# Order of ScalarE's Mish and of VectorE's sums in a fused linear attention and Mish MLP kernel

## The chip, the cores and the metric

The kernel runs on one NeuronCore of a Trainium2 chip. The metric is the time of one execution on the device, in microseconds. Engines are called as in the profile: PE is TensorE (PEld its weight loads), ACT is ScalarE, DVE is VectorE, POOL is GpSimd, and SP issues DMAs.

## What is computed

Decayed linear attention in blocks, with a state per batch and head, and then a two-layer MLP with Mish between the layers:

```python
B, H, S, D = 4, 8, 768, 64          # 3072 tokens, d_model 512, d_ff 2048
for b in range(S // 64):
    intra = einsum('bhij,bhjd->bhid', einsum('bhic,bhjc->bhij', qb, kb) * Dmask, vb)
    inter = einsum('bhid,bhde->bhie', qb * lam_pow, kv_state)
    out[:, :, block] = intra + inter
    kv_state = lam_block * kv_state + einsum('bhsd,bhse->bhde', kb * rev_pow, vb)
x = out.transpose(0, 2, 1, 3).reshape(B * S, H * D)
h = x @ w_in
g = h * tanh(log1p(exp(h)))         # Mish
return g @ w_out
```

Inputs and output are float32; the kernel works in float16 with float32 accumulation.

## The kernel before

**Periods.** The sequence is cut in six groups of 128 positions. A period n (0 to 5) takes one group of all four batches, 512 tokens, through the MLP, and works on the attention of the next group in between. Every engine's order is written out by hand: lists of `units`, and tables that say behind which unit u a token sum (`sums`), a transposition of q and k by DMA (`turns`), a load, or a part of the attention (`visit`) stands.

**First layer.** The hidden values are kept in hsg, 16 row blocks of 128 by 512 tokens. *Lower* tokens are the columns 0 to 255 (batches 0 and 1), *upper* ones 256 to 511. In period 0 (`mm1_unit`, L423) and period 1 all 16 row blocks are plain products. From period 2 on, row blocks 0 to 7 are plain: `mm1_duo(n, g, lo, hi)` (L444) makes two row blocks for one half of the tokens in one of the two PSUM banks of tag ph, and ACT applies Mish (L460). Row blocks 8 to 15 come from `set_unit` (L520), two sets g = 0, 1 of a scheme with seven block products instead of eight, P1 to P7. It needs sums of quarters of w_in (`in_sum`, made once in period 0) and of x (`x_sum`, L502: four DVE sums a period; P5 reads sum 0, P6 sum 1, P7 sum 2, P3 sum 3). Its steps, with the tiles that the profile names:

- P1 makes sx; ACT copies it to u (L576). P2 adds to sx; its Mish gives lower tokens, first columns.
- "open": ACT copies u into the bank of sz (L554), so that P6 adds to it.
- P5 makes sw; ACT copies it to p (L580).
- "mid": DVE adds sz and p into the bank of sy (L539).
- P7 adds to sz; DVE adds p into hs (L539); the Mish of hs (L535) gives upper tokens, second columns.
- P3 adds to sy; its Mish gives **lower** tokens, second columns.
- P4 adds to sz; its Mish gives **upper** tokens, first columns.

**Second layer.** `fast_unit` (L681) is the same scheme over hsg and w_out: tiles x, w, z, y, all made at L621. It needs sums of w_out (`weight_sum`, L471, tile tsum, made once in period 0) and of hsg (`token_sum`, L592, tile gsum, each in two parts, every period). Token sum 0 adds upper tokens of both halves of the row blocks; sum 1 takes from it lower tokens of row blocks 0 to 7; sum 2 uses row blocks 0 to 7 alone; sum 3 takes sum 1 from lower tokens of row blocks 8 to 15. The order in a period is P1 (x), P5 (w, reads sum 0), P6 (z, sum 1), P2 (x), P7 (z, sum 2), P3 (y, sum 3), P4 (z).

**Attention.** In `pair_s` (L338) PE makes the scores of two batches in four banks (tile pS, L349), and DVE masks them (tile sb, L365). `pair_o` (L368) multiplies by v; the result, xtok, is transposed by two DMAs from SP into xt (L392), which is what the next period's x sums and first layer read. In periods 2 to 4, the `pair_s` behind unit 3 stands just before the four x sums, which are behind unit 4. Up to the start of period 1 the scores are made batch by batch (`look_t`, `look_s`, L204 to L240) with transposes on PE (tiles pk, pq) and masks at L239.

**Pacing.** GpSimd delays loads of later groups: `pace` (L408) reads one element of the Mish output named last in `mark`.

Of the kernel before, what the change touches and what calls it, by code (L numbers as in the profile page):

```python
# [9 lines left out]
AF = mybir.ActivationFunctionType  # L10
# [10 lines left out]
def kernel(  # L21
# [10 lines left out]
    nc = tc.nc  # L32
# [408 lines left out]
        if hsg[n] is None:  # L441
            hsg[n] = work.tile([128, NKI, GT], F16, name="hsg", tag="hsg", bufs=2)

    def mm1_duo(n, g, lo, hi):  # L444

        new_hidden(n)
        h = GT // 2
        half = lo // h
        t = duo_bank(n, g, half)
        for m in range(2):  # L450
            ni = 2 * g + m
            for kc in range(NKC):
                nc.tensor.matmul(  # L453
                    t[:, m, lo - half * h : hi - half * h],
                    w_in(ni, kc),
                    xt[n][:, kc, lo:hi], start=(m == 0 and kc == 0), stop=(kc == NKC - 1),
                    skip_group_check=True,
                )
        if hi == half * h + h:
            nc.scalar.activation(hsg[n][:, 2 * g : 2 * g + 2, half * h : half * h + h], t, AF.Mish)  # L460
            mark.append(hsg[n][0:1, 2 * g, half * h : half * h + 1])

    HK = NKI // 2
    HN = DMO // 2
# [55 lines left out]
    def set_unit(n, g, step):  # L520

        def place(key):
            if (n, g, key) not in first:
                tag, bufs = homes[g][key]
                first[n, g, key] = ps.tile([128, 2, 2 * C], F32, name=f"s{key}{g}", tag=tag, bufs=bufs)
            return first[n, g, key]

        def kept(key):
            first[n, g, key] = work.tile([128, 2, 2 * C], F32, name=key, tag=key, bufs=2)
            return first[n, g, key]  # L530

        def mish(r, c, src):
            ni = NKI // 2 + 4 * g + 2 * c
            dst = hsg[n][:, ni : ni + 2, r * 2 * C : (r + 1) * 2 * C]
            nc.scalar.activation(dst, src, AF.Mish)  # L535
            mark.append(dst[0:1, 0, 0:1])

        def plus_p5(key, out):
            nc.vector.tensor_tensor(out=out, in0=first[n, g, key], in1=first[n, g, "p5"], op=ALU.add)  # L539

        def x_quarter(r, c):
            return lambda kk: xt[n][:, c * KH + kk, r * 2 * C : (r + 1) * 2 * C]

        def x_part(i):
            return lambda kk: xsum[n, i][:, kk, :]

        def w_quarter_(r, c):
            return lambda kk, m: i_quarter(g, r, c)[:, kk, m * 128 : (m + 1) * 128]

        def w_part_(i):  # L550
            return lambda kk, m: isum[g][i][:, kk, m * 128 : (m + 1) * 128]

        if step == "open":
            nc.scalar.activation(place("z"), first[n, g, "u1"], AF.Copy)  # L554
            return
        if step == "mid":
            plus_p5("z", place("y"))
            return
        key, lhs, rhs = {
            "P1": lambda: ("x", w_quarter_(0, 0), x_quarter(0, 0)),  # L560
            "P2": lambda: ("x", w_quarter_(1, 0), x_quarter(0, 1)),
            "P6": lambda: ("z", w_part_(1), x_part(1)),
            "P5": lambda: ("w", w_part_(0), x_part(0)),
            "P7": lambda: ("z", w_part_(2), x_part(2)),
            "P3": lambda: ("y", w_quarter_(1, 1), x_part(3)),
            "P4": lambda: ("z", w_part_(3), x_quarter(1, 1)),
        }[step]()
        t = place(key)
        for m in range(2):
            for kk in range(KH):  # L570
                nc.tensor.matmul(  # L571
                    t[:, m, :], lhs(kk, m), rhs(kk),
                    start=(step in ("P1", "P5") and m == 0 and kk == 0), stop=(kk == KH - 1),
                    skip_group_check=True)
        if step == "P1":
            nc.scalar.activation(kept("u1"), t, AF.Copy)  # L576
        elif step == "P2":
            mish(0, 0, t)
        elif step == "P5":
            nc.scalar.activation(kept("p5"), t, AF.Copy)  # L580
        elif step == "P7":
            o = work.tile([128, 2, 2 * C], F32, name="hs", tag="hs", bufs=2)
            plus_p5("z", o)
            mish(1, 1, o)
        elif step == "P3":
            mish(0, 1, t)
        elif step == "P4":
            mish(1, 0, t)

# [165 lines left out]
    units += [(fast_unit, (0, step, blk)) for step in ("P1", "P5") for blk in range(2)]  # L755
    units += [(fast_unit, (0, step, None, part)) for part in range(2) for step in ("P6", "P2")]
    units += [(fast_unit, (0, step, blk)) for step in ("P7", "P3", "P4") for blk in range(2)]
    sums = {3: ((2, 0),), 7: ((2, 1),), 11: ((0, 0), (1, 0), (3, 0)), 15: ((0, 1), (1, 1)), 16: ((3, 1),)}
    for u, (fn, args) in enumerate(units):
        put_off = []  # L760
        fn(*args, **({"then": put_off} if u in (23, 25) else {}))
        if u < B - 1:
            look_kv(u + 1, "pq" if u == 0 else "po")()
        if 8 <= u < 8 + NVB - B:
            nc.vector.memset(vz[u - 8 + B][:, :, D : 2 * D], 0.0)
        elif u == 13:
            nc.vector.tensor_scalar(out=maskT, in0=rel, scalar1=0.0, scalar2=None, op0=ALU.is_ge)
        for i, s in {14: ((0, 0),), 15: ((0, 1),), 18: ((1, 0), (2, 0)),
                     20: ((1, 1), (2, 1))}.get(u, ()):
            weight_sum(i, s)  # L770
        for i, part in sums.get(u, ()):
            token_sum(0, i, part)
        if u in (5, 8):
            for i in range(4):
                in_sum((u - 5) // 3, i)
        if u == 22:
            scale_k(4)
            weight_sum(3, 0)
        then = [f(i, "po" if i == 5 else "ph") if f is look_kv else f(i) for f, i in visit.get(u, ())]
        if u == 23:  # L780
            scale_k(5)
            scale_k(6)
            weight_sum(3, 1)
        for f in put_off + then:
            if f:
                f()
        if u in (25, 26, 27):
            for _ in range(2):
                ahead.pop(0)()
        if u == 26:  # L790
            scale_k(7)
    next_state(1, 0)

    for n in range(1, NG):
        r, s, t = Pair(), Pair(), Pair()
        r.n, r.bs, s.n, s.bs, t.n, t.bs = n, (2, 3), n + 1, (0, 1), n + 1, (2, 3)
        def duo(g, half):
            return mm1_duo, (n, g, half * (GT // 2), (half + 1) * (GT // 2))

        def part(g, *steps):  # L800
            return [(set_unit, (n, g, step)) for step in steps]
# [6 lines left out]
        if n == 1:  # L808
            units = [[duo(g, half)] for half in range(2) for g in range(NKI // 2)]
            visit = {11: (pair_s, s), 16: (pair_o, s), 21: (pair_a, s), 26: (pair_s, t), 29: (pair_o, t)}  # L810
            turns = {1: 9, 4: 10, 7: 11, 23: 12, 25: 13}
            slots = range(8, 16)
            sums = {9: ((2, 0),), 11: ((2, 1),), 13: ((0, 0), (1, 0)), 15: ((0, 1), (1, 1)), 20: ((3, 0),), 21: ((3, 1),)}
        else:
            units = [part(0, "P1") + part(1, "P1") + [duo(0, 0)], part(0, "P2") + part(1, "P2") + [duo(1, 0)],
                     [duo(2, 0)], [duo(3, 0)],
                     [duo(0, 1)], part(0, "open") + [duo(1, 1)], part(1, "open") + [duo(2, 1)],
                     part(0, "P5") + part(1, "P5"), part(0, "P6", "mid") + part(1, "P6"), [duo(3, 1)] + part(1, "mid"),
                     part(0, "P7") + part(1, "P7"), part(0, "P3") + part(1, "P3"),
                     part(0, "P4") + part(1, "P4")]  # L820
            if n == NG - 1:
                units[0] += units[1].pop(),
            visit = {}
            if n < NG - 1:
                visit = {0: (pair_a, r), 3: (pair_s, s), 13: (pair_o, s), 22: (pair_s, t), 25: (pair_o, t)}
            if n < NG - 2:
                visit[17] = pair_a, s
            turns = {1: (n + 1) * B + 2, 2: (n + 1) * B + 3, 20: (n + 2) * B, 23: (n + 2) * B + 1}
            slots = range(4, 16)
            sums = {9: ((2, 0),), 12: ((0, 0), (0, 1), (1, 0), (1, 1)), 14: ((2, 1),), 18: ((3, 0),), 19: ((3, 1),)}  # L830
# [3 lines left out]
        for u, calls in enumerate(units):  # L834
# [17 lines left out]
                token_sum(n, i, part)  # L852
            if turns.get(u, NG * B) < NG * B:
                turn(turns[u])
            if u in visit:
                f, s_ = visit[u]
                s_.spare = ("po", "po") if u < 13 else ("pS", "pk") if f is pair_a else ("ph", "po")
                if f is pair_o and s_ is s and n > 1:
                    f(s_, scales)
                else:  # L860
                    f(s_)
            if n > 1 and scales and u in (15, 16, 17, 19):
                scales.pop(0)()
            if n > 1 and u == 4:
                for i in range(4):
                    x_sum(n, i)


# [28 lines left out]
```

## Time and profile before

| | |
|---|---|
| median of 3 runs | 201.27 us (200.77 to 201.43) |
| the profiled execution's own time | 200.91 us |
| its span, first to last instruction | 199.1 us |
| granted TensorE clock | 1.0 of full speed |
| DMA moved | 26.82 MB |

The profile is of one execution; its span is 1.8 us shorter than that execution's time. In the timelines below a line gives the start, the length, the engine, the line of the kernel, the operation, output and inputs, shapes and a count; in brackets stands how long the engine was idle before it, and what ended that. Matmuls are pipelined: a row of eight lasts longer than the distance to the next group's start, so the text compares starts.

### The profile page before, as it was taken

The page shows a single profiled execution, that of the slowest core. Times are in us where ns is not written, and L with a number is a line of the kernel's source. Part 1 is how long each engine was busy: PE and PEld are TensorE (multiplying, and loading weights), DVE is VectorE, ACT ScalarE, POOL GpSimd, SP SyncE. Part 2 cuts the span into 40 slices and gives each one's busy share as a digit, 9 for nine tenths or more (in the row PEclk, how much of TensorE's full clock was granted, in tenths as well). Part 3 has the DMA queues.
Part 4 walks back from the last instruction along what each step waited for, and adds up shares of the span by engine and source line. Part 5 has one row for each costly group of instructions (what it writes and reads, how often), then busy time and mean ns, then how long its engine had stood idle before and what let it go on. Part 6 is the DMA issues. An engine that isn't in the chain of part 4 may idle for free.

```text
span 199.1 us, 5098 instructions
## 1 busy us (share of the span) xinstructions
PE 191.6 (96%) x2049; PEld 157.5 (79%) x2049; DVE 144.8 (73%) x279; ACT 110.8 (56%) x230; POOL 80.8 (41%) x129
## 2 busy tenths in 40 slices
PE   7978999999999999999999999999999999999993
PEld 3555447878888998988798988798988788888782
DVE  7689679799953978888589788589788538225813
ACT  5685665332665521567881557980657880787330
POOL 7996333679397810008980008970009000000000
PEclk9999999999999999999999999999999999999999
DMA  9999999999999996759999959999969714600014
GB/s 132 145 149 192 206 206 200 157 169 181 200 137 178 164 123 173 180 88 94 129 111 196 201 121 107 126 114 190 179 140 113 50 26 135 158 3 2 0 56 158
DMA packets 112458, 26.82 MB, mean 135 GB/s; under 512 B 101554, under 2 KB 112434, under 8 KB 112434
## 3 DMA queue, kind: packets, MB, share of 16 engines
q0 software_dynamic: 77552, 13.37, 91.7%
q1 hardware_dynamic: 30848, 9.97, 27.1%
q10 hardware_dynamic: 4034, 3.15, 5.6%
q8 instruction: 16, 0.26, 0.6%
q14 instruction: 8, 0.07, 0.1%
HBM read 27.26 MB, written 6.29 MB: 169 GB/s over the span
## 4 chain that ended last, share of the span: by engine, by line
PE 88%; ACT 5%; DVE 4%; issue 1%; ACTq 0%
PE ph L453 20%; PE z L621 14%; PE x L621 10%; PE ph L418 7%; PE w L621 6%; PE y L621 6%; PE sz L571 4%; PE sx L571 4%; PE pS L349 2%; PE pO L376 2%; PE pO L255 2%; PE sw L571 1%; ACT hsg L535 1%; PE pv L328 1%; PE sy L571 1%; PE busy L157 1%
## 5 line engine op out<-in xcount | busy, mean ns | idle before, releaser
L453 PE MATMUL ph<-xt,win 128*128 128x256 f16 x384 | 45.1, 273 | 0.0
L621 PEld LDWEIGHTS <-gsum 128*128 128x128 f16 x384 | 36.2, 98 | 7.3 <-DVE gsum L607 2.7
L453 PEld LDWEIGHTS <-win 128*128 128x128 f16 x384 | 37.1, 98 | 4.5
L460 ACT ACTIVATE hsg<-ph 128x512 f16<-128x512 f32 x48 | 28.6, 595 | 14.8 <-PE ph L453 14.6
L409 POOL COPY paced<-hsg 1x1 f16<-1x1 f16 x42 | 11.9, 284 | 54.8 <-ACT hsg L460 54.5
L621 PEld LDWEIGHTS <-hsg 128*128 128x128 f16 x272 | 26.0, 98 | 3.2
L607 DVE TENSOR_TENSOR gsum<-hsg 128x1024 f16<-128x1024 f16 x24 | 16.2, 688 | 14.2 <-ACT hsg L535 8.6
L621 PE MATMUL x<-wout,hsg 128*128 128x256 f16 x192 | 23.7, 273 | 0.0
L621 PE MATMUL z<-tsum,gsum 128*128 128x256 f16 x192 | 23.6, 273 | 0.0
L67 POOL DMA_DIRECT2D kn<-in_k_dram x23 | 20.5, 892 | 6.1 <-DMA win<-in_moe_w_in_dram 2.2
L78 POOL DMA_DIRECT2D vz<-in_v_dram x24 | 21.1, 884 | 4.3 <-DMA wout<-in_moe_w_out_dram 1.7
L75 POOL DMA_DIRECT2D qn<-in_q_dram x23 | 20.4, 886 | 6.0 <-DMA wout<-in_moe_w_out_dram 3.6
L365 DVE TENSOR_TENSOR sb<-pS,maskT 128x512 f16<-128x512 f32 x32 | 19.8, 683 | 1.9 <-PE pS L349 1.8
L678 ACT ACTIVATE osum<-z 128x512 f32<-128x512 f32 x5 | 3.0, 597 | 25.1 <-PE z L621 25.1
L265 DVE TENSOR_TENSOR ktil<-kn,lk 128x512 f16<-128x512 f16 (+1 forms) x22 | 14.6, 685 | 1.7 <-DMA kn<-in_k_dram 1.7
L288 DVE TENSOR_TENSOR raw<-pv,state 64x256 f32<-64x256 f32 x24 | 10.1, 422 | 6.5 <-PE pv L328 6.1
L418 PE MATMUL ph<-xt,win 128*128 128x512 f16 x64 | 14.5, 379 | 0.3 <-ACT xt L257 0.3
L571 PEld LDWEIGHTS <-isum 128*128 128x128 f16 x128 | 12.5, 97 | 2.1
L430 ACT ACTIVATE hsg<-ph 128x512 f16<-128x512 f32 x16 | 9.6, 597 | 5.8 <-PE ph L418 5.8
L621 PE MATMUL w<-tsum,gsum 128*128 128x256 f16 x96 | 12.2, 273 | 0.6 <-DVE gsum L607 0.4
L418 PEld LDWEIGHTS <-win 128*128 128x128 f16 x64 | 6.1, 98 | 7.3 <-issue 0.4
L621 PE MATMUL y<-wout,gsum 128*128 128x256 f16 x96 | 11.8, 273 | 0.0
(113 smaller groups left out, 307.9 us busy)
## 6 DMA issues: line engine op xcount, KB each, us to landing
vz<-in_v_dram POOLq DMA_DIRECT2D x24, 128.0 KB, 4.4
out_dram<-osum SPq DMA_DIRECT2D x12, 256.0 KB, 2.9
kn<-in_k_dram POOLq DMA_DIRECT2D x23, 128.0 KB, 5.0
qn<-in_q_dram POOLq DMA_DIRECT2D x23, 128.0 KB, 5.7
out_dram<-osum ACTq DMA_DIRECT2D x11, 256.0 KB, 3.1
wout<-in_moe_w_out_dram POOLq DMA_DIRECT2D x4, 512.0 KB, 16.1
win<-in_moe_w_in_dram POOLq DMA_DIRECT2D x3, 512.0 KB, 10.7
win<-in_moe_w_in_dram POOLq DMA_DIRECT2D x2, 256.0 KB, 6.8
```

What stands on the lines that cost most here:

```text
L67: nc.gpsimd.dma_start(out=kn[i], in_=chunk_rows(k, i))
L75: nc.gpsimd.dma_start(out=qn[i], in_=chunk_rows(q, i))
L78: nc.gpsimd.dma_start(out=vz[i % NVB][:, :, 0:D], in_=chunk_rows(v, i))
L265: (nc.gpsimd if B + 1 < i < 2 * B else nc.vector).tensor_tensor(out=t, in0=kn[i], in1=bc(lk, 2, D), op=ALU.mult)
L365: nc.vector.tensor_tensor(out=s.sb[m][t], in0=sc[m][t], in1=bc(maskT, 1, JP), op=ALU.mult)
L409: nc.gpsimd.tensor_copy(paced, mark[-1])
L418: nc.tensor.matmul(ph_t[ni][:, lo:hi], w_in(ni, kc), xt[n][:, kc, lo:hi], start=(kc == 0), stop=(kc == NKC - 1),)
L453: nc.tensor.matmul(t[:, m, lo - half * h : hi - half * h], w_in(ni, kc), xt[n][:, kc, lo:hi], start=(m == 0 and kc == 0), stop=(kc == NKC ...
L460: nc.scalar.activation(hsg[n][:, 2 * g : 2 * g + 2, half * h : half * h + h], t, AF.Mish)
L571: nc.tensor.matmul(t[:, m, :], lhs(kk, m), rhs(kk), start=(step in ("P1", "P5") and m == 0 and kk == 0), stop=(kk == KH - 1), skip_group_c ...
L607: nc.vector.tensor_tensor(out=gsum[n, i][:, ks, :], in0=a, in1=b, op=op)
L621: nc.tensor.matmul(places(n, key)[:, blk, lo:hi], lhs(kk, blk), rhs(kk, lo, hi), start=(fresh and kk == 0 and blk == 0), stop=(kk == HK - ...
```

## The change

Five edits; no operation is added or removed, only the place of some on ACT and DVE changes (and line numbers by up to 8). PE, POOL and SP issue the same instructions in the same order.

1. Periods 2 to 5: the Mish behind P3 (lower tokens, both sets) goes behind the Mish behind P4 (upper tokens, both sets).
2. Periods 2 to 5: the Mish of `mm1_duo` for row blocks 4 and 5, upper tokens, goes behind ACT's copy p of set 0.
3. Periods 2 to 4, where `pair_s` stands behind unit 3: x sum 0 is made before the masks of `pair_s`; sums 1 to 3 stay behind unit 4. In period 5 there are no masks, and the order of the sums stays.
4. Period 0: token sum 3, second part, goes from behind unit 16 to behind unit 21, on DVE behind four sums of w_out.
5. Period 0: `weight_sum(3, 1)` goes from behind the first `look_t` of unit 23 to unit 22.

```diff
-    def mm1_duo(n, g, lo, hi):
+    def mm1_duo(n, g, lo, hi, put_off=False):
...
-        if hi == half * h + h:
-            nc.scalar.activation(hsg[n][:, 2 * g : 2 * g + 2, half * h : half * h + h], t, AF.Mish)
-            mark.append(hsg[n][0:1, 2 * g, half * h : half * h + 1])
+        if hi == half * h + h and not put_off:
+            duo_mish(n, g, half)
+
+    def duo_mish(n, g, half):
+        h = GT // 2
+        dst = hsg[n][:, 2 * g : 2 * g + 2, half * h : half * h + h]
+        nc.scalar.activation(dst, duo_t[n, g, half], AF.Mish)
+        mark.append(dst[0:1, 0, 0:1])
...
+        if step == "late":
+            mish(0, 1, first[n, g, "y"])
+            return
...
-        elif step == "P3":
-            mish(0, 1, t)
...
-    sums = {3: ((2, 0),), 7: ((2, 1),), 11: ((0, 0), (1, 0), (3, 0)), 15: ((0, 1), (1, 1)), 16: ((3, 1),)}
+    sums = {3: ((2, 0),), 7: ((2, 1),), 11: ((0, 0), (1, 0), (3, 0)), 15: ((0, 1), (1, 1)), 21: ((3, 1),)}
...
         if u == 22:
             scale_k(4)
             weight_sum(3, 0)
+            weight_sum(3, 1)
...
             scale_k(6)
-            weight_sum(3, 1)
...
-                     [duo(0, 1)], part(0, "open") + [duo(1, 1)], part(1, "open") + [duo(2, 1)],
-                     part(0, "P5") + part(1, "P5"), part(0, "P6", "mid") + part(1, "P6"), [duo(3, 1)] + part(1, "mid"),
+                     [duo(0, 1)], part(0, "open") + [duo(1, 1)], part(1, "open") + [(mm1_duo, (n, 2, GT // 2, GT, True))],
+                     part(0, "P5") + [(duo_mish, (n, 2, 1))] + part(1, "P5"), part(0, "P6", "mid") + part(1, "P6"), [duo(3, 1)] + part(1, "mid"),
                      part(0, "P7") + part(1, "P7"), part(0, "P3") + part(1, "P3"),
-                     part(0, "P4") + part(1, "P4")]
+                     part(0, "P4") + part(1, "P4") + part(0, "late") + part(1, "late")]
...
+            if n > 1 and u == 3:
+                x_sum(n, 0)
             if u in visit:
...
             if n > 1 and u == 4:
-                for i in range(4):
+                for i in range(1, 4):
                     x_sum(n, i)
```

## Prediction

> **What bounds the kernel now.** I read the page first, then the waits of the weight loads, then the timelines of the engines around each place where TensorE stood still.
>
> ```profile
> span 199.1 us, 5098 instructions
> ...
> PE 191.6 (96%) x2049; PEld 157.5 (79%) x2049; DVE 144.8 (73%) x279; ACT 110.8 (56%) x230; POOL 80.8 (41%) x129
> ```
>
> ```profile
> PEld L621 <- DVE gsum L607: 2.7, 8, 0.7
> ```
>
> TensorE is busy for 96% of the span. No matmul is removed, so only its gaps can be won. The second answer, from the waits, names the largest repeated one: weight loads of the second product waited eight times for a sum of hidden tiles. For the rest I compare starts. Eight matmuls of 128x256 that wait for nothing take 0.87 us from start to start (91.63 to 92.51 below), 0.109 us each; what goes beyond is a gap.
>
> Period 5 shows the wait for the sum best: ScalarE, VectorE, TensorE.
>
> ```profile
> 181.52 1.23 ACT L535 ACTIVATE hsg<-hs 128x512 f16<-128x512 f32 x2 [0.69 <-DVE hs L539]
> 182.66 1.06 ACT L535 ACTIVATE hsg<-sy 128x512 f16<-128x512 f32 x2
> 183.61 1.09 ACT L535 ACTIVATE hsg<-sz 128x512 f16<-128x512 f32 x2
> ...
> 184.24 1.29 DVE L607 TENSOR_TENSOR gsum<-hsg 128x1024 f16<-128x1024 f16 x2 [2.16 <-ACT hsg L535]
> ...
> 182.66 1.91 PE L621 MATMUL x<-wout,hsg 128*128 128x256 f16 x16
> 184.99 2.09 PE L621 MATMUL w<-tsum,gsum 128*128 128x256 f16 x16 [0.42 <-DVE gsum L607]
> ```
>
> The sum reads the upper tokens' Mish, hs and sz; sy, the lower tokens', stands between them. The x matmuls would end at 182.66 + 16 x 0.109 = 184.41; w begins at 184.99, 0.58 late, and is 2.09 long against x's 1.91: another 0.18 for the sum's second half. Together 0.76 us.
>
> Period 2 is the pattern of periods 2 to 4: TensorE, VectorE, ScalarE.
>
> ```profile
> 88.03 2.79 PE L453 MATMUL ph<-xt,win 128*128 128x256 f16 x24
> 90.76 1.03 PE L571 MATMUL sw<-xsum,isum 128*128 128x256 f16 x8
> 91.63 1.04 PE L571 MATMUL sz<-xsum,isum 128*128 128x256 f16 x8
> 92.51 1.04 PE L453 MATMUL ph<-xt,win 128*128 128x256 f16 x8
> ...
> 95.17 1.08 PE L571 MATMUL sz<-xt,isum 128*128 128x256 f16 x8
> ...
> 97.43 1.04 PE L621 MATMUL x<-wout,hsg 128*128 128x256 f16 x8
> 98.51 1.76 PE L621 MATMUL w<-tsum,gsum 128*128 128x256 f16 x13
> ...
> 87.89 2.49 DVE L365 TENSOR_TENSOR sb<-pS,maskT 128x512 f16<-128x512 f32 x4 [0.59 <-PE pS L349]
> 90.30 0.42 DVE L514 TENSOR_TENSOR xsum<-xt 128x512 f16<-128x512 f16 x1
> ...
> 97.76 1.29 DVE L607 TENSOR_TENSOR gsum<-hsg 128x1024 f16<-128x1024 f16 x2 [2.16 <-ACT hsg L535]
> ...
> 89.88 0.60 ACT L554 ACTIVATE sz<-u 128x512 f32<-128x512 f32 x1 [0.17 <-DVE sb L365]
> ...
> 90.89 0.59 ACT L554 ACTIVATE sz<-u 128x512 f32<-128x512 f32 x1
> 91.41 0.58 ACT L460 ACTIVATE hsg<-ph 128x512 f16<-128x512 f32 x1
> 91.89 1.08 ACT L580 ACTIVATE p<-sw 128x512 f32<-128x512 f32 x2
> ```
>
> x would end at 97.43 + 0.87 = 98.30; w begins 0.21 later and, with the same two halves of a sum as in period 5, loses the same 0.18 inside: 0.39. The ph group would end at 88.03 + 24 x 0.109 = 90.65; sw, which reads the first x sum (begun at 90.30, behind the masks), begins 0.11 later. The row at 95.17 is 1.08 where its like has 1.04: 0.05 of waiting for VectorE; the sz group before it I take as the same.
>
> Third, the boundary of periods 0 and 1: VectorE, TensorE.
>
> ```profile
> 34.82 0.68 DVE L480 TENSOR_TENSOR tsum<-wout,tsum 128x1024 f16<-128x1024 f16 x1
> ...
> 37.92 0.69 DVE L480 TENSOR_TENSOR tsum<-wout,tsum 128x1024 f16<-128x1024 f16 x1
> 39.71 0.69 DVE L219 TENSOR_TENSOR pqT<-pq,lq 128x512 f16<-128x512 f16 x1 [1.11 <-PE pq L211]
> ...
> 40.92 0.69 DVE L480 TENSOR_TENSOR tsum<-wout,tsum 128x1024 f16<-128x1024 f16 x1
> 41.52 1.28 DVE L239 TENSOR_TENSOR sb<-pS,maskT 128x512 f16<-128x512 f32 x2
> ...
> 33.67 1.91 PE L621 MATMUL w<-tsum,gsum 128*128 128x256 f16 x16
> 35.56 1.05 PE L621 MATMUL z<-tsum,gsum 128*128 128x256 f16 x8
> ...
> 40.81 1.05 PE L621 MATMUL z<-tsum,gsum 128*128 128x256 f16 x8
> 42.26 0.38 PE L211 MATMUL pk<-ident,ktil 128*128 128x128 f16 x4 [0.40 <-DVE sb L239]
> ```
>
> w would end at 35.42; z begins 0.14 later, after the sum of w_out of 34.82. The z of 40.81 would end at 41.68; pk begins 0.58 later, when the first mask (41.52) has read that bank. Ahead of the masks stands the sum of w_out of 40.92.
>
> **The change part by part.**
>
> *Sums of period 0.* weight_sum(3, 1), 0.69 us, goes from 40.92 to behind 37.92, into the 1.11 us for which VectorE waits at 39.71: hidden. The hidden sum that stands just ahead of 34.82 goes behind the four sums of w_out after it; its reader y comes after 42.26: hidden. One such sum holds VectorE for 0.60 us (40.92 to 41.52), so that of 34.82 begins 0.6 earlier and the 0.14 goes. The masks begin 0.6 earlier, and pk at about 41.69 instead of 42.26: 0.57 goes. Next in line there is the second mask, done just as pO wants it. Together -0.71.
>
> *Lower tokens' Mish last.* sz takes sy's slot, 0.95 earlier (182.66 for 183.61), so the sums begin at 183.29 and 183.9, and w at 184.41 waits for neither: -0.76. P4's matmuls, which sz reads, stand ahead of x and end by 182.9; the second sz comes after that. In periods 2 to 4 the sums move to 96.8 and 97.4 against a w due at 98.30: -0.39 each. Late now is sy, by about 1.1 us; its readers P2 and the last token sum come after w (in period 5 after 186.7; sy ends at 184.7). Its banks pk and ph are next written even later. POOL's pacing reads an earlier mark in two units of a period, so two loads may go a little sooner; no row shows TensorE waiting for a load after period 1, so I cost it at nothing, at most 0.1 either way.
>
> *Mish of duo(2, 1) behind a copy.* No row shows this order. The copy p takes the slot of 91.41, the Mish runs from 91.90 to 92.48, and its ph bank is needed by the ph group that would now begin at 92.40 (92.51 less the 0.11). TensorE follows a release by 0.06 (w at 98.51 after a sum that ends at 97.76 + 0.69), so 92.54: **a new wait of +0.15**, bounds 0 and 0.3. The second copy stays in its place; the additions on VectorE behind the first come sooner, so the two 0.05 go. In period 5 there are no masks ahead and I take +0.05, bounds 0 and 0.15.
>
> *First x sum ahead of masks.* sw's 0.11 goes. But VectorE is in order: behind a first sum that waits for xt wait the masks, behind them ScalarE's sz (0.17 <-DVE sb) and the Mish after it, and TensorE's banks. When does xt land? SP's timeline, the landing of the two transposes in each of periods 3 and 4, and VectorE:
>
> ```profile
> 82.21 2.72 SPq L392 DMA_TRANSPOSE xt<-xtok  x2
> ...
> 113.19 2.52 SPq L392 DMA_TRANSPOSE xt<-xtok  x2
> ...
> 143.16 2.52 SPq L392 DMA_TRANSPOSE xt<-xtok  x2
> ...
> DMA to landing us min/median/max: 2.4/2.4/2.4
> ...
> 117.41 2.48 DVE L365 TENSOR_TENSOR sb<-pS,maskT 128x512 f16<-128x512 f32 x4 [0.59 <-PE pS L349]
> ...
> 146.93 2.49 DVE L365 TENSOR_TENSOR sb<-pS,maskT 128x512 f16<-128x512 f32 x4 [0.59 <-PE pS L349]
> ...
> 173.65 0.43 DVE L514 TENSOR_TENSOR xsum<-xt 128x512 f16<-128x512 f16 x1 [3.58 <-DMA xt<-xtok]
> ```
>
> The second transpose is issued 1.3 us after the first and lands 2.4 later: 116.9 and 146.9. Add 0.1 for the wait to end and 0.35 to 0.42 for the sum: masks could begin at 117.4 (they began at 117.41: no loss) and 147.3 (146.93: **+0.4**). In period 2 the same steps give 82.21 + 1.3 + 2.4 = 85.9, and VectorE, idle for 0.59 us ahead of 87.89, has room for the sum: no loss. So +0.4 in all, bounds 0 and 1.2 (0.4 in each).
>
> The Trainium skill, TensorE: Matmul & The Clock Gate, § Architectural detail, has ScalarE and VectorE as strict first-in-first-out queues. The last row, where VectorE sat 3.58 us at a sum, agrees; by that rule this edit costs masks whenever xt is late.
>
> **The sum.** Boundary -0.71; periods 2 to 4 each -0.39 - 0.11 - 0.10 + 0.15 = -0.45, together -1.35; late xt +0.4; period 5 -0.76 + 0.05 = -0.71. In all -2.37. The profiled execution took 200.91 us, 1.8 more than its span, and would take 198.5; it lies 0.36 under the median of 201.27. From the median I get 198.9.
>
> **The rivals.**
>
> 1. *Late xt in every period, and a bit of the boundary lost.* Landing moves with DMA load, and half a microsecond later than now is enough. For it: only 0.0 and -0.4 us of room in periods 3 and 4. Masks 0.4 late three times and half of the boundary's 0.71 gone: gain 2.37 - 0.8 - 0.35 = 1.2, so 200.1.
>
> 2. *Period 1 eats the boundary's gain.* If the transposes that feed period 1's scores land by DMA time and not by TensorE's, -0.71 becomes a wait there: 199.6. For it: xt's landing above shows that a transposition is 2.4 us or more behind its issue, and there the queue also feeds every score. Against: the waits of TensorE and of its weight loads name no transposed q or k.
>
> 3. *Slower: the masks held for long.* The same place as rival 1, with another size. The other parts gain 2.77, so the change loses when the three periods' masks are held by more than 0.92 us each; at 1.2 us each, 201.27 - 2.77 + 3.6 = 202.1. Against: TensorE's own ph group right after the scores (88.03) reads the same columns of xt, and it shows no wait now.
>
> 4. *The gap at w is a bank and not the sum.* Then reordering sz leaves 3 x 0.39 + 0.76 = 1.93 of it, and the gain is 0.44: 200.8. Against: the sums' end (98.45) and w's start (98.51) fit each other. The Trainium skill, Perfetto Trace Analysis, § Optimization Strategy, says that the same gap repeating can mean too little PSUM; the releaser named in the rows speaks for data here, but by that rule my new +0.15 at ph is what to expect of a bank held longer.
>
> **How the numbers follow.** Forecast 0.62, rival 1 0.14, rival 2 0.10, rival 3 0.06, rival 4 0.08. A measurement of this kernel tells 0.3%, 0.6 us, from no change. Faster than 200.67: forecast, rivals 1 and 2, together 0.86; rival 4 (200.8) and what lies about it gives same 0.08; slower 0.06. The range: below, no mask delay and no bank wait, 198.9 - 0.4 - 0.5 = 198.0; above, rival 1's 200.1. It leaves out rivals 3 and 4 and the tails. Forecast's own range: 198.0 to 199.5.
>
> **What would show it.** Boundary: pk follows z without a gap, tsum no longer stands before the masks. Lower Mish: ScalarE's order hs, sz, sy, token sums near 0.95 us sooner, the waits' row of eight for gsum gone or under 1 us. Put-off Mish: a short gap of 0.1 to 0.2 at the ph group behind sz in periods 2 to 4, ended by ScalarE. First x sum: sw right behind ph, xsum ahead of sb; where "<-DMA xt" stands before that xsum, sb is late by as much. I am wrong if the gap at w stays, if sb is late by over 0.5 us in several periods, or if a new wait for kraw or qraw stands in period 1.

## The result and the profile after

The changed kernel takes **199.32 us** (median of 19 runs, 198.09 to 200.63), the kernel before 200.91 us (19 runs, 200.13 to 202.39). The ratio is 0.992, 95% interval 0.9897 to 0.9943: 1.6 us less, between 1.1 and 2.1. Where a run lay over 1.5% above the fastest of its kernel (one of e8 below, 202.86 us, and one of the kernel before beside it, 203.35 us), the ratios leave it out. The profiled execution took 198.38 us, its page begins so:

```profile
span 196.6 us, 5100 instructions
...
PE 189.4 (96%) x2049; PEld 157.8 (80%) x2049; DVE 145.2 (74%) x279; ACT 110.7 (56%) x230; POOL 78.7 (40%) x129
```

The busy times of VectorE and ScalarE are as before; 2.2 us of TensorE's are gone. (Its matmuls overlap, 0.27 us long and 0.109 apart, so most of a short gap counts as busy.) Lines of the kernel moved: 480 is now 485, 607 is 613, 621 is 627, 535 is 540, 514 is 519, 460 is 465, 554 is 559, 571 is 579, 580 is 588; in the experiments they differ by a few.

**Period 5**, from the timelines of ScalarE, VectorE and TensorE:

```profile
180.89 1.07 ACT L540 ACTIVATE hsg<-sz 128x512 f16<-128x512 f32 x2
181.85 1.09 ACT L540 ACTIVATE hsg<-sy 128x512 f16<-128x512 f32 x2
...
181.50 1.29 DVE L613 TENSOR_TENSOR gsum<-hsg 128x1024 f16<-128x1024 f16 x2 [1.18 <-ACT hsg L540]
...
180.86 1.91 PE L627 MATMUL x<-wout,hsg 128*128 128x256 f16 x16
182.60 1.91 PE L627 MATMUL w<-tsum,gsum 128*128 128x256 f16 x16
```

sz now comes ahead of sy. The sum starts at 181.50, its second half is done at 182.8, and w follows x after 1.74 us, which is 16 x 0.109: no bracket stands behind w, and it is 1.91 long like x. The row of eight waits for gsum no longer stands among the waits of the weight loads.

**Period 2**, TensorE, VectorE, ScalarE:

```profile
86.92 2.79 PE L453 MATMUL ph<-xt,win 128*128 128x256 f16 x24
89.56 1.04 PE L579 MATMUL sw<-xsum,isum 128*128 128x256 f16 x8
90.43 1.04 PE L579 MATMUL sz<-xsum,isum 128*128 128x256 f16 x8
91.43 1.03 PE L453 MATMUL ph<-xt,win 128*128 128x256 f16 x8
...
96.26 1.04 PE L627 MATMUL x<-wout,hsg 128*128 128x256 f16 x8
97.14 1.04 PE L627 MATMUL w<-tsum,gsum 128*128 128x256 f16 x8
...
86.12 0.42 DVE L519 TENSOR_TENSOR xsum<-xt 128x512 f16<-128x512 f16 x1
86.79 2.48 DVE L365 TENSOR_TENSOR sb<-pS,maskT 128x512 f16<-128x512 f32 x4 [0.25 <-PE pS L349]
...
88.77 0.60 ACT L559 ACTIVATE sz<-u 128x512 f32<-128x512 f32 x1 [0.17 <-DVE sb L365]
...
90.78 0.60 ACT L465 ACTIVATE hsg<-ph 128x512 f16<-128x512 f32 x1
```

w is right behind x, and sw behind ph. The new wait is there as well: from sz to ph 1.00 us pass, where eight matmuls take 0.87. The 0.13 ends 0.05 after the put-off Mish of 90.78, which is done at 91.38: the fifth of ScalarE's operations back to back since it got a mask at 88.77. Here xt is in time: the masks wait for the scores, not for the sum.

**Period 4**, SP, VectorE, ScalarE, TensorE:

```profile
141.25 2.52 SPq L392 DMA_TRANSPOSE xt<-xtok  x2
...
145.09 0.42 DVE L519 TENSOR_TENSOR xsum<-xt 128x512 f16<-128x512 f16 x1 [0.76 <-DMA xt<-xtok]
145.55 2.48 DVE L365 TENSOR_TENSOR sb<-pS,maskT 128x512 f16<-128x512 f32 x4
...
147.53 0.60 ACT L559 ACTIVATE sz<-u 128x512 f32<-128x512 f32 x1 [0.72 <-DVE sb L365]
148.06 0.58 ACT L465 ACTIVATE hsg<-ph 128x512 f16<-128x512 f32 x1
...
147.75 0.60 PE L579 MATMUL sw<-xsum,isum 128*128 128x256 f16 x4
148.70 0.60 PE L579 MATMUL sw<-xsum,isum 128*128 128x256 f16 x4 [0.34 <-ACT hsg L465]
```

This is the late xt, read from top to bottom: the sum waits for the transpose, the masks stand behind the sum, ScalarE's sz waits 0.72 us for a mask instead of 0.17, the Mish behind it frees its bank late, and sw stops in its middle, since the second set's sw is written into a bank of tag ph: four matmuls should take 0.44 and take 0.95.

**The boundary of periods 0 and 1**, VectorE, TensorE:

```profile
35.58 0.69 DVE L485 TENSOR_TENSOR tsum<-wout,tsum 128x1024 f16<-128x1024 f16 x1 [0.88 <-DMA wout<-in_moe_w_out_dram]
...
36.79 0.69 DVE L613 TENSOR_TENSOR gsum<-hsg,gsum 128x1024 f16<-128x1024 f16 x1
...
38.00 1.28 DVE L485 TENSOR_TENSOR tsum<-wout,tsum 128x1024 f16<-128x1024 f16 x2
39.20 0.68 DVE L219 TENSOR_TENSOR pqT<-pq,lq 128x512 f16<-128x512 f16 x1
...
38.69 1.04 PE L627 MATMUL z<-tsum,gsum 128*128 128x256 f16 x8
39.94 0.40 PE L234 MATMUL pS<-pqT,pkT 64*128 64x128 f16 x8 [0.21 <-DVE pqT L219]
40.27 1.05 PE L627 MATMUL z<-tsum,gsum 128*128 128x256 f16 x8
41.15 0.39 PE L211 MATMUL pk<-ident,ktil 128*128 128x128 f16 x4
```

pk follows the z of 40.27 after 0.88 us: its wait is gone. But ahead of pS there is a new one, and it was in no row of before: from z to pS pass 1.25 us, where before they were 0.97 (39.51 to 40.48). The token sum of 36.79 and the second of the two sums at 38.00 are the moved ones; with them VectorE no longer idles ahead of pqT, and pS is 0.28 late.

**Where the time went, by periods.** For each kernel, in us: from the first w of a period to that of the next; the first of these stretches with the wait at its z for a sum of w_out taken out (beyond 0.87 us from x to z, shown by itself); and from the last w to the end of the span. The kernels e0 to e10 are the experiments below.

| | wait at z | 0 to 1, rest | 1 to 2 | 2 to 3 | 3 to 4 | 4 to 5 | to the end |
|---|---|---|---|---|---|---|---|
| before | 0 | 35.50 | 29.34 | 29.52 | 29.51 | 27.45 | 14.14 |
| after | 0 | 35.07 | 29.07 | 29.06 | 29.69 | 26.71 | 13.98 |
| e0 | 0.16 | 35.49 | 29.33 | 29.51 | 29.68 | 27.44 | 14.13 |
| e1 | 0.66 | 35.49 | 29.13 | 29.13 | 29.13 | 26.69 | 13.97 |
| e2 | 1.05 | 35.49 | 29.33 | 29.51 | 29.51 | 27.44 | 14.14 |
| e3 | 0.51 | 35.23 | 29.34 | 29.51 | 29.51 | 27.45 | 14.13 |
| e4 | 0.12 | 35.23 | 29.14 | 29.14 | 29.55 | 26.68 | 13.96 |
| e5 | 0.52 | 35.24 | 29.07 | 29.07 | 29.10 | 26.71 | 13.98 |
| e8 | 0.25 | 35.24 | 29.30 | 29.31 | 32.09 | 26.71 | 13.96 |
| e9 | 1.04 | 35.49 | 29.07 | 29.06 | 29.37 | 26.71 | 13.96 |
| e10 | 0.38 | 34.78 | 29.07 | 29.07 | 29.07 | 26.71 | 13.98 |
| e6 | 0.13 | 34.78 | 28.97 | 28.96 | 28.96 | 26.71 | 13.95 |

From before to after the columns give -1.88 us. The spans differ by 2.55; the other 0.67 lies ahead of the first w (at 33.67 and 33.00). That w begins anywhere between 32.82 and 34.00 in these twelve executions, and the earliest instruction that an edit moves, a token sum that ran at 34.21 in before, comes after it: the 0.67 isn't the change's.

### The profile page after: what moved, and what is told of

It is laid out like the page before. It is cut to its first block, busy times and chain, and to the rows that moved or that the text cites. A ratio compares the mean times of both kernels' runs of the same rounds, so it can differ in the third digit from the quotient of the medians.

```text
span 196.6 us, 5100 instructions
## 1 busy us (share of the span) xinstructions
PE 189.4 (96%) x2049; PEld 157.8 (80%) x2049; DVE 145.2 (74%) x279; ACT 110.7 (56%) x230; POOL 78.7 (40%) x129
## 4 chain that ended last, share of the span: by engine, by line
PE 74%; DMA 11%; POOL 8%; DVE 4%; issue 1%; ACT 1%; POOLq 0%; DVEq 0%; ACTq 0%
PE ph L453 19%; PE z L627 14%; DMA wout<-in_moe_w_out_dram 10%; PE x L627 9%; PE y L627 6%; PE sz L579 5%; PE w L627 4%; PE sx L579 3%; PE pS L349 2%; PE pO L376 2%; POOL win L93 2%; POOL vz L78 2%; PE sy L579 2%; PE sw L579 2%; POOL kn L67 1%; POOL qn L75 1%
## 5 line engine op out<-in xcount | busy, mean ns | idle before, releaser
L627 PEld LDWEIGHTS <-gsum 128*128 128x128 f16 x384 | 36.9, 98 | 4.5
L409 POOL COPY paced<-hsg 1x1 f16<-1x1 f16 x42 | 9.8, 234 | 55.3 <-ACT hsg L465 55.3
L654 DVE TENSOR_TENSOR osum<-z,p 128x512 f32<-128x512 f32 x6 | 4.1, 690 | 10.6 <-issue 5.9
## 6 DMA issues: line engine op xcount, KB each, us to landing
wout<-in_moe_w_out_dram POOLq DMA_DIRECT2D x4, 512.0 KB, 16.4
```

The lines of the kernel that those rows point to most:

```text
L627: nc.tensor.matmul(places(n, key)[:, blk, lo:hi], lhs(kk, blk), rhs(kk, lo, hi), start=(fresh and kk == 0 and blk == 0), stop=(kk == HK - ...
```

## The experiments

**e0, the order of before in the new code.** The control: all five edits undone, with the code split as in the changed kernel.

> All five edits undone in the changed file: every engine has the order of before. Theory and rivals: no difference, within 0.3 us. If it differs by more, that is what a build by itself can shift, and the other runs are to be read with that.

Measured: 201.10 us (12 runs), before 200.95; ratio 1.0004 (0.998 to 1.0029). What the columns say comes from the order, not from the splitting. Its stretch 3 to 4 is 0.17 over that of before; TensorE stood still there for 0.16 and 0.21 ahead of sx and ph, which read xt.

**e1, edit 1 alone** (lower tokens' Mish last), beside the kernel before:

```diff
-        elif step == "P3":
-            mish(0, 1, t)
...
-                     part(0, "P4") + part(1, "P4")]
+                     part(0, "P4") + part(1, "P4") + part(0, "late") + part(1, "late")]
```

> Only lower tokens' Mish last (edit 1). Theory (the gap at w is the wait for the token sum, and the sum comes 0.95 us sooner): no gap at w in periods 2 to 5, -0.39 three times and -0.76, in all -1.9 us, 199.0 from 200.9; sw still 0.11 late behind the x sum. Rival (the gap is a bank): the gap at w stays and the time with it, within 0.3 us of before.

Measured: 199.57 us, before 200.78; ratio 0.9935 (0.9909 to 0.9961). TensorE in period 2:

```profile
97.49 1.04 PE L627 MATMUL x<-wout,hsg 128*128 128x256 f16 x8
98.36 0.82 PE L627 MATMUL w<-tsum,gsum 128*128 128x256 f16 x6
```

w is 0.87 behind x: the gap closes by this order alone, with the same banks. The table has -0.21, -0.39, -0.38, -0.76 and -0.17 in the five columns behind the boundary, -1.91 in all. The gap was the sum and not a bank: rival 4 falls. (w has a count of 6 because the view ends at 99.) The medians lie 1.2 us apart, 0.8 to 1.8 by the interval: less than the 1.91 of the columns, and 199.57 is 0.6 over the 199.0 expected. No column shows this difference, and it stays open.

**e2, edit 3 alone** (first x sum ahead of the masks), beside the kernel before:

```diff
+            if n > 1 and u == 3:
+                x_sum(n, 0)
...
-                for i in range(4):
+                for i in range(1, 4):
```

> Only the first x sum ahead of the masks (edit 3). Theory: sw follows ph without its 0.11 us in periods 2 and 3, but the masks are held in period 4 by 0.4 to 0.6 us behind a landing of xt, and the hold goes through ScalarE's sz to TensorE: net between -0.1 and +0.4 us. Rival (the hold is covered, since the gaps at w behind it take it up): -0.3 us. Rival (masks held in every period): over +0.9 us.

Measured: 201.51 us (12 runs); ratio 1.0033 (1.0014 to 1.0052), so slower. TensorE in period 2:

```profile
89.20 2.80 PE L453 MATMUL ph<-xt,win 128*128 128x256 f16 x24
91.84 1.04 PE L576 MATMUL sw<-xsum,isum 128*128 128x256 f16 x8
...
94.46 1.18 PE L576 MATMUL sz<-xsum,isum 128*128 128x256 f16 x8
95.48 1.04 PE L576 MATMUL sy<-xsum,win 128*128 128x256 f16 x8
```

sw comes 2.64 behind ph, without the 0.11. But sz now takes 1.02 to the next group where before it took 0.92 (93.38 to 94.30), and the stretches are those of before to 0.01 us: the wait moved three groups on. In this execution the columns behind the boundary give 0, so the 0.6 us of the median aren't explained by them. The wait for w_out at z, 1.05 here, could be it; one profile can't show that, and it stays open, as for e1.

**e3, edits 4 and 5 alone** (period 0), beside the kernel before:

```diff
-    sums = {..., 15: ((0, 1), (1, 1)), 16: ((3, 1),)}
+    sums = {..., 15: ((0, 1), (1, 1)), 21: ((3, 1),)}
...
             weight_sum(3, 0)
+            weight_sum(3, 1)
...
             scale_k(6)
-            weight_sum(3, 1)
```

> Only the moved sums of period 0 (edits 4 and 5). Theory: the 0.58 us ahead of pk goes, and 0.14 ahead of z, where w_out has landed in time: -0.4 to -0.7 us, with period 1 as long as before. Rival (the gain is eaten in period 1 by landings of transposed q and k): start of w in period 1 sooner by under 0.2 us against the start of w in period 0, and a wait for kraw or qraw.

Measured: 200.69 us (12 runs); ratio 0.9998 (0.9976 to 1.0019). VectorE and TensorE:

```profile
36.07 0.69 DVE L485 TENSOR_TENSOR tsum<-wout,tsum 128x1024 f16<-128x1024 f16 x1 [1.54 <-DMA wout<-in_moe_w_out_dram]
...
39.69 0.69 DVE L219 TENSOR_TENSOR pqT<-pq,lq 128x512 f16<-128x512 f16 x1
...
36.82 1.03 PE L626 MATMUL z<-tsum,gsum 128*128 128x256 f16 x8 [0.34 <-DVE tsum L485]
...
40.43 0.40 PE L234 MATMUL pS<-pqT,pkT 64*128 64x128 f16 x8 [0.31 <-DVE pqT L219]
```

The time did not move, where 0.4 to 0.7 us less were expected. The stretch without the wait at z is 0.26 shorter, not 0.71: pS is 0.37 late (39.09 to 40.43, where 0.97 would do), and the first pk 0.07.

**e9, the changed kernel with edits 4 and 5 taken back.** The same lines, the other way round.

> The changed kernel with edits 4 and 5 taken back. Theory A (the two moves in period 0 only carry the wait from the matmuls pk to the scores pS, so they are worth nothing on the whole): within 0.3 us of the changed kernel's median of 199.3, with the wait of about 0.57 us ahead of pk back and none ahead of pS. Rival B (they are worth the 0.43 us by which the stretch from the w of period 0 to that of period 1 was shorter in the profiled execution): 199.8. Periods 2 to 5 as in the changed kernel: 29.1, 29.1, 29.1 to 29.7 and 26.7 us from w to w.

Measured: 198.92 us (5 runs, 198.78 to 199.56); ratio 0.9904 (0.9884 to 0.9924). VectorE and TensorE:

```profile
40.13 0.69 DVE L219 TENSOR_TENSOR pqT<-pq,lq 128x512 f16<-128x512 f16 x1 [0.64 <-PE pq L211]
...
42.68 0.38 PE L211 MATMUL pk<-ident,ktil 128*128 128x128 f16 x4 [0.40 <-DVE sb L239]
```

pk waits again, pS no longer; VectorE idles for 0.64 ahead of pqT. The time is 0.4 below that of the changed kernel, a little more than the 0.3 of theory A, and far from the 199.8 of rival B: the two edits gain nothing that the times show. The table's 0.25 lies within what the two intervals leave open.

**e4, the changed kernel without edit 2** (no Mish put off):

```diff
-                     part(0, "P5") + [(duo_mish, (n, 2, 1))] + part(1, "P5"), ...
+                     part(0, "P5") + part(1, "P5"), ...
```

> All but the Mish put off behind the copy (edit 2 undone). Theory: the 0.13 us ahead of the ph group behind sz goes in periods 2 to 4, and the two gaps of 0.05 us behind it that edit 2 had removed come back: within 0.3 us of the changed kernel, -1.6 to -2.4 us from before. Rival (edit 2 is a part of the gain): slower than the changed kernel by over 0.3 us.

Measured: 199.40 us (6 runs); ratio 0.9922 (0.9891 to 0.9953), like the changed kernel's, as expected. In period 2 the wait ahead of ph is gone, and the groups of sz behind it wait 0.15 and 0.05 us instead. In the table, edit 2 is worth 0.07 and 0.08 where xt is in time (29.14 twice, against 29.07 and 29.06).

**e5, the changed kernel without edit 3** (all x sums behind the masks):

```diff
-            if n > 1 and u == 3:
-                x_sum(n, 0)
...
-                for i in range(1, 4):
+                for i in range(4):
```

> All but the first x sum ahead of the masks (edit 3 undone). Theory: with edit 2 the ph group behind sz waits for ScalarE's line whatever sw does, so sw's 0.11 us comes back and the wait ahead of ph shrinks by as much; the hold of the masks in period 4 goes. From w to w 29.1 us in each of periods 2 to 4, and 0.3 to 0.6 us faster than the changed kernel. Rival (edit 3 is a part of the gain): slower than the changed kernel by 0.3 us.

Measured: 198.69 us (6 runs); ratio 0.9881 (0.9848 to 0.9914). VectorE and TensorE in period 4:

```profile
145.74 2.48 DVE L365 TENSOR_TENSOR sb<-pS,maskT 128x512 f16<-128x512 f32 x4 [0.59 <-PE pS L349]
...
146.03 2.78 PE L453 MATMUL ph<-xt,win 128*128 128x256 f16 x24
148.64 1.04 PE L579 MATMUL sw<-xsum,isum 128*128 128x256 f16 x8
```

The masks wait only for the scores. Periods 2 and 3 take what they take in the changed kernel, to 0.01 us, and period 4 takes 0.59 less. Edit 3 gains nothing where xt is in time and loses where it is late. The medians lie 0.6 apart with intervals that overlap; the columns carry the verdict.

**e8, the suspected cost made larger**: the changed kernel with the sums 0 and 1 ahead of the masks.

```diff
             if n > 1 and u == 3:
                 x_sum(n, 0)
+                x_sum(n, 1)
```

> The changed kernel with a second x sum, 0.42 us, ahead of the masks as well: the suspected cost doubled. Theory: what the masks are held goes to TensorE in full, +0.1 us in period 2 (which had 0.25 us of room), +0.4 in periods 3 and 4: from w to w 29.2, 29.5 and 30.1 us, 0.8 to 1 us slower than the changed kernel. Rival (the hold is taken up by slack on ScalarE or in the banks): under 0.3 us.

Measured: 200.55 us (12 runs); ratio 0.9976 (0.995 to 1.0001): 1.2 us over the changed kernel, near the 0.8 to 1 expected. Periods 2 and 3 are 0.23 and 0.25 longer (expected 0.1 and 0.4), so a second sum costs even where xt is in time. Period 4 is longer by 2.40, but that isn't the sums' alone, and the execution profiled, 201.93 us, lies 1.4 above the median. TensorE:

```profile
140.48 1.05 PE L579 MATMUL sx<-xt,win 128*128 128x256 f16 x8 [0.66 <-DMA xt<-xtok]
...
148.24 2.78 PE L453 MATMUL ph<-xt,win 128*128 128x256 f16 x24 [1.12 <-DMA xt<-xtok]
```

Here both transposes were so late that TensorE itself waited for them.

**e10, the changed kernel with the x sums back and another order in period 0.** Behind the landing of w_out's last quarter come first the two sums that read it; the token sum and a sum of w_out that don't read it go ahead of it.

```diff
-    sums = {..., 21: ((3, 1),)}
+    sums = {..., 18: ((3, 1),)}
...
-        for i, s in {14: ((0, 0),), 15: ((0, 1),), 18: ((1, 0), (2, 0)),
+        for i, s in {14: ((0, 0),), 15: ((0, 1),), 18: ((1, 0), (2, 0), (3, 0)),
...
-            weight_sum(3, 0)
             weight_sum(3, 1)
```

> The changed kernel with the x sums back behind the masks, and with the one thing of period 0 changed that the traces blame: behind the landing of the last quarter of w_out, VectorE does only the two sums that read it; the sum of w_out and the token sum that do not read it go ahead of that landing. Theory A (that landing and what stands behind it on VectorE set the boundary): no wait ahead of pS or pk, 34.9 to 35.1 us from the w of period 0 to that of period 1, and 0.4 to 0.6 us less than the kernel with the x sums alone put back (198.7), so 198.2. Rival B (what the best kernel so far gains beyond 198.7 comes from its order of masks): 198.7, and a boundary of 35.4 us or more.

Measured: 198.36 us (6 runs); ratio 0.9874 (0.985 to 0.9898). VectorE and TensorE:

```profile
39.21 0.69 DVE L219 TENSOR_TENSOR pqT<-pq,lq 128x512 f16<-128x512 f16 x1 [0.64 <-PE pq L211]
...
39.01 1.04 PE L627 MATMUL z<-tsum,gsum 128*128 128x256 f16 x8
39.98 0.40 PE L234 MATMUL pS<-pqT,pkT 64*128 64x128 f16 x8
40.31 1.05 PE L627 MATMUL z<-tsum,gsum 128*128 128x256 f16 x8
41.19 0.39 PE L211 MATMUL pk<-ident,ktil 128*128 128x128 f16 x4
```

Neither pS nor pk waits, and VectorE has its 0.64 of room back. The stretch is 34.78 without the wait at z, 0.71 below that of before: what I had forecast for the boundary. The time is 0.33 below e5's, within both intervals; with the wait at z the stretch was 35.16, a little over the 34.9 to 35.1 expected.

**e6, the best version**: edits 1 and 2, the period 0 of e10, and in periods 2 to 4 masks in the order (0,0), (1,0), (1,1), (0,1) with x sum 0 between the third and the fourth.

```diff
+        for m, t in ((0, 0), (1, 0), (1, 1), (0, 1)) if early else ...:
+            if early and (m, t) == (0, 1):
+                early()
...
+                    f(s_, lambda: x_sum(n, 0))
```

> A version for the causes found. Edits 1 and 2 stay. In pair_s of periods 2 to 4 the mask whose bank sz needs is made first, and the first x sum stands ahead of the last mask only. In period 0 the sum of w_out that needs no late quarter, and the last token sum, stand before the sums that wait for the last quarter of w_out. Theory: no gap at sw, ph and w in periods 2 to 4, from w to w 28.9 us each; period 0 no longer than in the changed kernel when w_out lands late. 0.5 to 1 us faster than the changed kernel, 198.3 to 198.9 where before takes 200.8. Rival (time from w_out's landing sets the start and nothing behind it helps): period 0 as before, and the gain is that of periods 2 to 5 alone, -2.3 us.

Measured: **197.74 us** (6 runs, 197.36 to 198.23); ratio 0.9837 (0.9808 to 0.9866), below both kernels. VectorE and TensorE in period 2:

```profile
87.41 1.89 DVE L366 TENSOR_TENSOR sb<-pS,maskT 128x512 f16<-128x512 f32 x3 [0.37 <-PE pS L349]
89.22 0.42 DVE L520 TENSOR_TENSOR xsum<-xt 128x512 f16<-128x512 f16 x1
...
87.77 2.79 PE L454 MATMUL ph<-xt,win 128*128 128x256 f16 x24
90.40 1.04 PE L580 MATMUL sw<-xsum,isum 128*128 128x256 f16 x8
91.27 1.04 PE L580 MATMUL sz<-xsum,isum 128*128 128x256 f16 x8
92.17 1.03 PE L454 MATMUL ph<-xt,win 128*128 128x256 f16 x8
```

The masks wait for the scores and xt has 1.8 us more to land. sw has no gap, and ph 0.03 instead of 0.13: another 0.10 a period. What the order of the masks and what the sum's later place give of it wasn't run apart. The columns from the first stretch (without z's wait) to the end add up to 3.13 less than before's; the medians differ by 3.2.

## Why the prediction was right, and where a size was off

The sign, the time (199.32 for 198.9) and the range held. That the time came so near is in part luck: the sum of -2.37 was taken off 201.27, a median of 3 runs, and the median of 19 is 200.91, from which it gives 198.5. The gain measured, 1.6, is two thirds of the one forecast. The forecast mechanism is the one that the traces show, except for two things: the sums of period 0, and what edits 2 and 3 gain each. In us, the sum as forecast and as the columns have it:

| term | forecast | measured |
|---|---|---|
| sums of period 0 | -0.71 | -0.25 (e3 to e5, e8); -0.43 in the profile of after |
| lower Mish last, periods 2 to 5 | -1.93 | -1.91 (e1) |
| sw, two short waits, new bank wait | -0.06 a period | -0.06 and -0.07 (after against e1, periods 2 and 3) |
| late xt | +0.4, all in period 4 | +0.59 in after, all in period 4 |
| put-off Mish, period 5 | +0.05 | +0.02 (after against e1) |

1. **Lower Mish last.** Right at each place: e1 has 0.21 + 0.18 a period and 0.76 for period 5, and nobody waits for sy. By the Trainium skill (Perfetto Trace Analysis, § Optimization Strategy) a repeating gap can mean too little PSUM; e1 closes this one with the banks unchanged, so here the trace speaks against that reading. For the 0.13 at ph, a bank held longer, it agrees.

2. **Put-off Mish.** The new wait came out at 0.13 for 0.15, behind the engine that was named. But I had booked this edit at +0.05 a period (-0.10 and +0.15), and it is what gains the 0.06: e5 has it without edit 3, and its periods 2 and 3 take 29.07 for e1's 29.13.

3. **First x sum.** The place and the size of the loss were right. In the four kernels that make this sum alone first, the stretch 3 to 4 shows 0 (e2), 0.30 (e9), 0.41 (e4) and 0.59 (after) over their like without it, and the loss follows xt: counted from the w of period 3, its second half landed at 18.23, 18.47, 18.59 and 18.80 us, and where there is a loss the masks began 0.55 after that.

   The transfer itself was never slow: in period 4 of all twelve executions this half landed 2.4 to 2.6 us after its issue. What moved was the issue, from 15.3 to 18.3 us after that w, although the last xtok was written by 13.5. So xt is late because of what SP works off ahead of it, and not, as rival 1 supposed, because its landing moves with DMA load; what holds up SP wasn't tried.

   The queue in order, cited in the prediction from the Trainium skill (TensorE: Matmul & The Clock Gate, § Architectural detail), shows here from VectorE to ScalarE to TensorE. But the -0.11 that I booked as this edit's gain is none: without edit 3 (e5, period 2) sw waits 0.12 and ph 0.04, with it ph waits 0.13. sw's wait is for the sum, but the start of ph is set by ScalarE's chain behind the masks, which the sum does not move: what sw gains, ph loses (from the first mask to ph it is 4.65 us in e5 and 4.64 in after). The period's sum came out right because I had booked the bank wait beside it, a gain too much on edit 3 against one too little on edit 2: that is luck.

4. **Sums of period 0: the step that failed.** "goes from 40.92 to behind 37.92, into the 1.11 us for which VectorE waits at 39.71: hidden", and of the token sum, "its reader y comes after 42.26: hidden". Each move was weighed alone. Both sums now stand between w_out's landing and pqT, and two of 0.60 don't fit into 1.11, still less into the 0.64 that is left when w_out lands later (e9). The token sum had stood ahead of that landing, where VectorE now sits idle for 0.88 us. So the wait of 0.57 ahead of pk went, and 0.37 and 0.07 came back ahead of pS and pk (e3). I had also asked of the token sum only when its own reader wants it, not which instructions behind it on VectorE it pushes back. Edits 4 and 5 weren't run apart.

5. **The rivals.** Rival 1 is refuted in its main part by the executions profiled: masks were late in one period, not in three. Its other part, about half of the boundary's gain lost, is what came. Rival 2's shape was right and its place wrong: a landing ate part of the boundary's gain, but that of w_out in period 0, and not of q and k in period 1, which stand in no wait there. Rival 3's price per period, over 0.92 us, isn't reached by one sum; e8, with two, is not slower than before either. Rival 4 is refuted by e1.

6. **From the profile to the median.** The profiled execution gained 2.5 us and the median 1.6. Of the difference, 0.67 lies ahead of the first w. So that the profiled 198.38 meets the 198.5 of the forecast is luck as well. With -0.25 for -0.43 at the boundary the columns would give 1.7, which agrees with 1.6; this is an estimate, since the wait at z and the late xt differ from execution to execution too.

## What to carry to other kernels

Moves into one idle stretch share it: add them up against the shortest stretch that the executions show, and ask of each moved instruction what waits behind it on its engine, not only who reads it. Behind a load whose landing varies, put first only what reads that load; whatever does not goes ahead of it. A wait that goes away on an engine paced by another engine's chain comes back a few groups later, unless the move shortens that chain.

## What the runs showed of the hardware

The last quarter of w_out, issued by GpSimd between 16.4 and 18.0 us, landed between 35.56 and 37.73 us in twelve executions, 2.4 to 3.9 us after the first w. Nothing that an edit moves runs ahead of that issue. The five kernels with before's order in period 0 have mostly later landings (36.08 to 37.73, against 35.56 to 36.36 in the five with edits 4 and 5); five against five don't tell chance from a cause. The z that needs it began 0.77 us after the landing wherever it waited (36.05 to 36.82 in e3, 36.97 to 37.74 in e9), and lost 0 to 1.05 us by it. That is more than most of the gains looked for here, so columns with this wait taken out told kernels apart where medians of 5 to 12 runs did not. Why it varies wasn't tried.
